# Reordering the first loads of a fused attention + token-mixing kernel: the first chunk of x as two column halves on two queues, and chunk 2 scaled in halves

## The chip, the cores and the metric

One core of a Trainium2 chip. The metric is the device time of one execution, in microseconds (us), lower is better; a profile gives the *span*, from the first to the last instruction of the program, which is some 2 us shorter than the time. All numbers are of fast runs (granted TensorE clock 1.0) unless said otherwise.

Names: PE is TensorE, DVE is VectorE, ACT is ScalarE, POOL is GpSimd, SP is SyncE, whose instruction stream issues most of the DMAs here. A load *lands* when the trace shows its completion.

## The reference, cut to what matters

```python
xn = _layernorm(x)                       # x: 2048 tokens x 1024, bf16
out = x + attention(xn, wq, wk, wv, wo, beta) + mixer(xn, w1, b1, w2, b2)

def mixer(x, w1, b1, w2, b2):            # mixes over the tokens
    h = _layernorm(x)
    u = gelu(einsum('bsd,sf->bdf', h, w1) + b1)     # contraction over the 2048 tokens
    y = einsum('bdf,fs->bds', u, w2) + b2
    return y.transpose(0, 2, 1)
```

What matters is the start of the mixer. The contraction runs over tokens, so the kernel takes x in 16 *chunks* of 128 tokens: chunk c must be loaded, its mean and variance found, its 1024 columns normalised to `h`, and then 8 matmuls (4 pieces of 128 columns of `w1`, times 2 halves of `h`) may use it.

## The kernel before: the parts that matter

The first loads, all issued from SP. Every `load_x` is 256 KB a chunk (128 rows of 2 KB), every `load_w1` 128 KB a chunk (rows of 1 KB).

```python
def loads(self):
    ...                                            # two memsets on GpSimd
    fw.op("act", lambda e: e.activation(..., ACT.Gelu_apprx_tanh), ...)   # loads the table early
    self.load_x(0, 1)
    self.load_x(1, 1)
    self.load_w1(0, 2)                             # chunks 0 and 1
    self.load_x(2, 1)
    self.load_x(3, 1)
    self.load_w1(2, 2)
    ...                                            # and so on
```

The statistics of chunks 1, 2, 4, 6, ... are two passes on ScalarE (one for the mean, one for the mean square); those of chunks 0, 3, 5, ... are `bn_stats` on VectorE. `scale` is two or three small operations (on GpSimd, but for chunk 0's first), the last a power of -0.5; `ln_h` is the normalisation on VectorE.

```python
ACT_STATS = (1, 2, 4, 6, 8, 10, 12, 14)

def norm_and_first_hidden(self):
    self.stats(0); self.scale(0)
    self.stats(1)
    self.ln_h(0, 0); self.ln_h(0, 1)               # in halves of 512 columns
    self.scale(1)
    self.ln_h(1, 0); self.ln_h(1, 1)
    self.early_hidden(0)                           # 8 matmuls
    self.stats(3)
    for c in self.ACT_STATS[1:]:
        self.stats(c)
    self.early_hidden(1)
    for c in range(2, N_TCH, 2):
        self.scale(c); self.ln_h(c)                # whole, 1024 columns
        if c + 3 < N_TCH: self.stats(c + 3, 0)
        self.scale(c + 1); self.ln_h(c + 1)
        if c + 3 < N_TCH: self.stats(c + 3, 1)
        ...
        self.early_hidden(c); self.early_hidden(c + 1)
```

In the traces here each engine works through its own instructions in the order in which they are written (in `hold_w1` below, VectorE waits until 9.23 us for chunk 3 and comes to chunk 2 at 10.57, although chunk 2's power is ready at 9.90). While the data arrives, 14 dummy matmuls keep TensorE busy.

The softmax here doesn't subtract the row's maximum and nothing guards it: scores larger than these inputs give would overflow.

## Time and profile before

| | before |
|---|---|
| time, median of 4 fast runs in the rounds of the comparison | 694.65 us (694.49 to 694.68) |
| span of the profiled run | 693.0 us |
| TensorE busy | 687.8 us, 99% |
| real matmuls begin | 6.58 us |
| TensorE's wait before chunk 2 | 1.02 us |
| chunk 2's first matmul | 11.22 us |

From the profile's page of the kernel before: span, busy time of each engine with its share of the span, and the chain of work that ended last by engine.

```profile
span 693.0 us, 11585 instructions
PE 687.8 (99%) x4822; PEld 329.1 (47%) x4822; DVE 268.4 (39%) x602; ACT 282.0 (41%) x513; POOL 118.2 (17%) x235
PE 98%; DMA 1%; ACT 0%; SPq 0%; DVE 0%; issue 0%
```

TensorE is the limit everywhere but in the first 12 us. The timeline of TensorE there (kernel before; columns: start, duration, engine, line, what, and in brackets the idle time before it and what ended it):

```profile
6.58 3.61 PE L217 MATMUL ps_all<-h,w1all 128*128 128x512 bf16 x16 [0.54 <-DVE h L836]
11.22 5.12 PE L217 MATMUL ps_all<-h,w1all 128*128 128x512 bf16 x23 [1.02 <-DVE h L836]
```

Chunks 0 and 1 are the 16 matmuls of the first line; then TensorE waits for the normalised chunk 2. The chain that ended last, in order of time (kernel before; columns: start, duration, what), says why:

```profile
2.19 4.92 DMA xin<-in_A_x_dram
...
7.14 1.16 ACT xn_tmp L800 x2
8.32 1.15 ACT xn_tmp L802 x2
9.47 1.05 ACT xn_tmp L800 x2
10.52 0.56 DVE h L836
11.22 662.61 PE ps_all L217 x4605
```

Chunk 2 of x, the fourth DMA, is issued at 2.19 us and lands at 7.12; ScalarE's two passes over it end at 9.47; then `h`, then 662 us of TensorE in one piece. One step is mislabelled. A wait is put down to the engine that came last, and the 1.05 us "ACT L800" is ScalarE's next pass, on another chunk. What really stands between ScalarE's end and VectorE's start is GpSimd, as its timeline line (kernel before) shows: a power that ends at 10.38, after a subtract that waited for ScalarE.

```profile
9.82 0.56 POOL L828 TENSOR_TENSOR ln_r<-ln_t,mhalf 128x1 f32<-128x1 f32 x1
```

ScalarE's timeline (kernel before) shows what released it: chunk 1's landing, then, after a pause of 0.68 us, chunk 2's.

```profile
4.13 1.06 ACT L800 ACTIVATE xn_tmp<-xin 128x1024 bf16<-128x1024 bf16 x1 [1.84 <-DMA xin<-in_A_x_dram]
...
6.28 0.19 ACT L802 ACTIVATION_READ_ACCUMULATOR xn_tmp<-xin 128x1 f32 x1
7.14 1.06 ACT L800 ACTIVATE xn_tmp<-xin 128x1024 bf16<-128x1024 bf16 x1 [0.68 <-DMA xin<-in_A_x_dram]
```

### The profile page before, as it was taken

How to read it: one execution, taken by the hardware profiler on the slowest of the kernel's cores; microseconds unless marked ns; L12 is line 12 of the kernel's file. 1: busy time of each engine (PE TensorE's matmuls, PEld its weight loads, DVE VectorE, ACT ScalarE, POOL GpSimd, SP SyncE). 2: the span in 40 equal slices, each digit the busy share in tenths (PEclk: the TensorE clock that was granted, in tenths of full speed). 3: DMA queues.
4: the chain of work that ended last, by engine and by line, in shares of the span. 5: the costliest groups of instructions: out<-in, count | busy, mean ns of one | idle time of the engine just before them, and what ended most of it. 6: DMA issues, size and time to landing. Idle time of an engine off the chain costs nothing.

```text
span 693.0 us, 11585 instructions
## 1 busy us (share of the span) xinstructions
PE 687.8 (99%) x4822; PEld 329.1 (47%) x4822; DVE 268.4 (39%) x602; ACT 282.0 (41%) x513; POOL 118.2 (17%) x235
## 2 busy tenths in 40 slices
PE   8999999999999999999999999999999999999998
PEld 3444444444444544545445454444445454444544
DVE  6731100000002433434555464655556463453545
ACT  7331111111136364454544525354543525443450
POOL 5810000000001221211212112121212212121230
PEclk9999999999999999999999999999999999999999
DMA  9377666323038445456272644526263442424114
GB/s 318 109 172 184 161 155 202 99 61 101 1 103 186 104 93 135 94 120 137 46 146 61 137 78 100 123 53 144 55 146 81 95 110 53 116 61 113 37 26 147
DMA packets 211325, 77.32 MB, mean 112 GB/s; under 512 B 173898, under 2 KB 203594, under 8 KB 211274
## 3 DMA queue, kind: packets, MB, share of 16 engines
q1 hardware_dynamic: 211274, 76.59, 44.7%
q8 instruction: 38, 0.62, 0.4%
q14 instruction: 13, 0.11, 0.1%
HBM read 59.79 MB, written 5.24 MB: 94 GB/s over the span
## 4 chain that ended last, share of the span: by engine, by line
PE 98%; DMA 1%; ACT 0%; SPq 0%; DVE 0%; issue 0%
PE ps_all L217 98%; DMA xin<-in_A_x_dram 1%; ACT xn_tmp L800 0%; SPq L245 0%; ACT xn_tmp L802 0%; DVE h L836 0%; DVE fin L1254 0%
## 5 line engine op out<-in xcount | busy, mean ns | idle before, releaser
L217 PE MATMUL ps_all<-gT,w2h 128*128 128x512 bf16 x896 | 229.0, 379 | 0.0
L1072 ACT ACTIVATE pT<-ps_all 128x512 bf16<-128x512 f32 x320 | 161.9, 617 | 111.3 <-PE ps_all L217 111.3
L217 PE MATMUL ps_all<-h,w1all 128*128 128x512 bf16 x896 | 193.7, 379 | 1.6 <-DVE h L836 1.6
L1080 POOL TENSOR_SCALAR_AFFINE_SELECT pT<-pT 128x256 bf16<-128x256 bf16 (+3 forms) x176 | 91.8, 527 | 545.0 <-ACT pT L1072 541.1
L217 PEld LDWEIGHTS ps_all<-h,w1all 128*128 128x128 bf16 x896 | 87.5, 98 | 107.7 <-issue 1.5
L217 PEld LDWEIGHTS ps_all<-gT,w2h 128*128 128x128 bf16 x896 | 79.9, 97 | 82.6 <-issue 7.8
L950 ACT ACTIVATE gT<-ps_all,bc 128x512 bf16<-128x512 f32 x56 | 37.7, 690 | 141.4 <-PE ps_all L217 141.4
L1118 DVE CAST ost<-ps_all 128x264 bf16<-128x264 f32 (+1 forms) x128 | 50.5, 396 | 80.4 <-PE ps_all L217 79.7
L217 PEld LDWEIGHTS ps_all<-vA,pT 128*128 128x128 bf16 x1280 | 50.3, 96 | 29.6 <-POOL pT L1080 0.5
L217 PE MATMUL ps_all<-xnT,wq 128*128 128x512 bf16 x256 | 60.5, 379 | 0.0
L217 PE MATMUL ps_all<-xnT,wk 128*128 128x512 bf16 x256 | 60.5, 379 | 0.0
L217 PE MATMUL ps_all<-wv_sb,xnT 128*128 128x512 bf16 x256 | 60.1, 379 | 0.0
L217 PE MATMUL ps_all<-vA,pT 128*128 128x33 bf16 x1280 | 51.7, 178 | 0.0
L977 DVE CAST qT<-ps_all 128x512 bf16<-128x512 f32 x29 | 20.1, 692 | 79.8 <-PE ps_all L217 79.8
L976 ACT ACTIVATE vA<-ps_all 128x512 bf16<-128x512 f32 x18 | 10.8, 599 | 90.6 <-PE ps_all L217 90.6
L888 DVE TENSOR_SCALAR gcol<-gcol 128x32 f32<-128x32 f32 x1 | 0.2, 181 | 118.6 <-ACT gcol L886 118.6
L217 PEld LDWEIGHTS ps_all<-wv_sb,xnT 128*128 128x128 bf16 x256 | 25.1, 98 | 30.2
L217 PEld LDWEIGHTS ps_all<-xnT,wk 128*128 128x128 bf16 x256 | 25.0, 98 | 30.2
L217 PEld LDWEIGHTS ps_all<-xnT,wq 128*128 128x128 bf16 x256 | 25.0, 98 | 30.1 <-issue 0.2
L976 ACT ACTIVATE kT<-ps_all 128x512 bf16<-128x512 f32 x32 | 19.1, 597 | 37.6 <-PE ps_all L217 37.6
L217 PE MATMUL ps_all<-wo_sb,oT 128*128 128x512 bf16 x128 | 34.3, 379 | 0.0
L961 DVE TENSOR_SCALAR etmp<-etmp 128x512 bf16<-128x512 bf16 x48 | 17.6, 367 | 39.0 <-ACT etmp L960 39.0
(68 smaller groups left out, 424.2 us busy)
## 6 DMA issues: line engine op xcount, KB each, us to landing
w2h<-in_B_w_dram SPq DMA_DIRECT2D x64, 224.0 KB, 3.2
w1all<-in_B_w_dram SPq DMA_DIRECT2D x12, 1024.0 KB, 5.3
wq<-in_A_wq_dram SPq DMA_DIRECT2D x32, 256.0 KB, 2.9
wk<-in_A_wk_dram SPq DMA_DIRECT2D x32, 256.0 KB, 2.9
stg<-in_A_x_dram SPq DMA_DIRECT2D x16, 256.0 KB, 3.8
out_dram<-stg SPq DMA_DIRECT2D x16, 256.0 KB, 2.9
xin<-in_A_x_dram SPq DMA_DIRECT2D x5, 512.0 KB, 7.4
w1all<-in_B_w_dram SPq DMA_DIRECT2D x8, 256.0 KB, 6.5
```

The source lines that it names most:

```text
L217: ins = self.nc.tensor.matmul(out, *args, **kwargs)
L888: fw.op("dve", lambda e: e.tensor_scalar(self.gcol[:], self.gcol[:], 1.0, None, op0=ALU.add), reads=[self.R_gcol], writes=[self.R_gcol])
L950: fw.op("act", lambda e: e.activation(self.gT[:, fc, half * 512:(half + 1) * 512], self.bank(b), ACT.Gelu_apprx_tanh, bias=self.b1c[:, fc: ...
L961: fl.op({"dve": (lambda e: e.tensor_scalar(et[:], et[:], 1.0, None, op0=ALU.min), 294, 330)}, [R_et], [R_et], prio=2)
L976: self.flow.op({"act": (lambda e, b: e.activation(dst, view(self.bank(b)), ACT.Copy), 635, 560), "dve": (lambda e, b: e.tensor_copy(dst, v ...
L977: "dve": (lambda e, b: e.tensor_copy(dst, view(self.bank(b))), 690, 727)},
L1072: fl.op({"act": (lambda e, b, slot=slot: e.activation(pT[:, slot, :], self.bank(b), ACT.Exp, scale=SCALE), 620, 530)}, [], [R[slot]], box= ...
L1080: fl.op({"pool": (lambda e, ap=ap, pat=pat: e.affine_select(ap, ap, pattern=pat, compare_op=ALU.is_ge, fill=0.0, base=0, channel_multiplie ...
L1118: fl.op({"dve": (lambda e, b: e.tensor_copy(dst, self.ps[:, b, 0:n * VW]), 150 + n * 35, 185 + n * 35)}, [], [self.R_ost[o][qb]], box=box, ...
```

## The change

The intent is to start the real matmuls sooner and to close the wait before chunk 2: chunk 0 arrives as two column halves issued at once from SP and from ScalarE; chunk 1 follows on ScalarE's queue; the first `w1` pieces come singly, so chunk 2 stands further ahead; chunk 2 is normalised, and taken by TensorE, in halves.

```diff
+        for half, issuer in ((0, "sp"), (1, "act")):
+            cols = slice(512 * half, 512 * half + 512)
+            fw.dma(self.xin[:, 0, cols], self.x_d[:, 0, cols], writes=[self.R_x0[half]], issuer=issuer)
+        self.load_x(1, 1, "act")
         fw.op("act", ... ACT.Gelu_apprx_tanh ...)
-        self.load_x(0, 1)
-        self.load_x(1, 1)
-        self.load_w1(0, 2)
+        self.load_w1(0, 1)
         self.load_x(2, 1)
+        self.load_w1(1, 1)
         self.load_x(3, 1)
+        self.load_x(4, 1)
         self.load_w1(2, 2)
 ...
         self.early_hidden(0)
-        self.stats(3)
         for c in self.ACT_STATS[1:]:
             self.stats(c)
+        self.stats(3, 0)
+        self.stats(3, 1, False)          # without the aggregate
+        self.scale(2)
+        self.ln_h(2, 0)
+        self.ln_h(2, 1)
+        self.aggregate(3)
         self.early_hidden(1)
         for c in range(2, N_TCH, 2):
-            self.scale(c)
-            self.ln_h(c)
+            if c > 2:
+                self.scale(c)
+                self.ln_h(c)
 ...
-        order = ... if c < 2 else \
+        order = ... if c < 3 else \      # half by half, so the first 4 matmuls need one half of h
```

(The rest is bookkeeping: which wait belongs to which half of chunk 0.)

More of the change, by code (lines that the diff above doesn't have):

```diff
@@ L632, in alloc @@
         self.R_xin = [Res(f"xin{c}") for c in range(N_TCH)]
+        self.R_x0 = [Res(f"x0_{half}") for half in range(2)]
         self.R_xnt = [Res(f"xnt{i}") for i in range(4)]
@@ L640, in over_early @@
         e = _Arena(self.nc, self.early_base, self.early_end)
-        wait = _after(*self.R_xin, *self.R_xnt)
+        wait = _after(*self.R_xin, *self.R_x0, *self.R_xnt)
         self.wv_sb = e.take("wv_sb", [P, N_DCH, D_MODEL], BF16)
@@ L717, in loads @@
         fw.op("pool", lambda e: e.memset(self.brow[:], 0.0), writes=[self.R_brow, self.R_brow2])
+        for half, issuer in ((0, "sp"), (1, "act")):
+            cols = slice(512 * half, 512 * half + 512)
+            fw.dma(self.xin[:, 0, cols], self.x_d[:, 0, cols], writes=[self.R_x0[half]], issuer=issuer)
+        self.load_x(1, 1, "act")
         fw.op("act", lambda e: e.activation(self.ln_t[:, 0, 0:1], self.mhalf[:, 0:1], ACT.Gelu_apprx_tanh),
               reads=[self.R_mhalf], writes=[self.R_st[0]], ns=1500)
-        self.load_x(0, 1)
-        self.load_x(1, 1)
-        self.load_w1(0, 2)
+        self.load_w1(0, 1)
         self.load_x(2, 1)
+        self.load_w1(1, 1)
         self.load_x(3, 1)
+        self.load_x(4, 1)
         self.load_w1(2, 2)
-        for c in range(4, 16, 2):
-            if c == 4:
-                self.load_x(4, 1)
-                self.load_x(5, 1)
-            else:
-                self.load_x(c, 2)
+        self.load_x(5, 1)
+        self.load_w1(4, 2)
+        for c in range(6, 16, 2):
+            self.load_x(c, 2)
             self.load_w1(c, 2)
@@ L742, in loads, with load_x, xin_half @@
         self.w1_next = 3
-    def load_x(self, c0, n):
+    def load_x(self, c0, n, issuer="sp"):
         self.fw.dma(self.xin[:, c0:c0 + n, :], self.x_d[:, c0:c0 + n, :],
-                    writes=[self.R_xin[c] for c in range(c0, c0 + n)])
+                    writes=[self.R_xin[c] for c in range(c0, c0 + n)], issuer=issuer)
+    def xin_half(self, c, half):
+        return self.R_x0[half] if c == 0 else self.R_xin[c]
     def load_w1(self, c0, n, issuer="sp"):
@@ L789, in norm_and_first_hidden, with stats @@
             self.early_hidden(c + 1)
-    def stats(self, c, part=None):
+    def stats(self, c, part=None, whole=True):
         fw = self.fw
@@ L806, in stats, with aggregate @@
         if part != 1:
-            fw.op("dve", lambda e: e.bn_stats(st[:, 0:6], src[:, 0:512]), reads=[self.R_xin[c]], writes=[R_t], ns=690)
+            fw.op("dve", lambda e: e.bn_stats(st[:, 0:6], src[:, 0:512]), reads=[self.xin_half(c, 0)], writes=[R_t], ns=690)
         if part != 0:
-            fw.op("dve", lambda e: e.bn_stats(st[:, 6:12], src[:, 512:1024]), reads=[self.R_xin[c], R_t], writes=[R_t],
+            fw.op("dve", lambda e: e.bn_stats(st[:, 6:12], src[:, 512:1024]), reads=[self.xin_half(c, 1), R_t], writes=[R_t],
                   ns=690)
-            fw.op("dve", lambda e: e.bn_aggr(self.ln_mv[:, c, :], st.rearrange("p (a s) -> p a s", s=6)),
-                  reads=[R_t], writes=[self.R_mean[c], self.R_var[c]])
+            if whole:
+                self.aggregate(c)
+    def aggregate(self, c):
+        st = self.ln_st[:, c, :]
+        self.fw.op("dve", lambda e: e.bn_aggr(self.ln_mv[:, c, :], st.rearrange("p (a s) -> p a s", s=6)),
+                   reads=[self.R_st[c]], writes=[self.R_mean[c], self.R_var[c]])
     def scale(self, c):
@@ L833, in ln_h @@
         a, z = (0, D_MODEL) if half is None else (512 * half, 512 * half + 512)
-        for hf in ((0, 1) if half is None else (half,)):
-            assert self.R_h[c][hf] is not None
         fw.op("dve", lambda e: e.tensor_scalar(self.h[:, c, a:z], self.xin[:, c, a:z], self.ln_mv[:, c, 0:1],
                                                self.ln_r2[:, c:c + 1], op0=ALU.subtract, op1=ALU.mult),
-              reads=[self.R_xin[c], self.R_mean[c], self.R_rs[c]],
+              reads=[self.xin_half(c, hf) for hf in ((0, 1) if half is None else (half,))]
+              + [self.R_mean[c], self.R_rs[c]],
               writes=self.R_h[c] if half is None else [self.R_h[c][half]], ns=(z - a) // 2 + 30)
@@ L843, in early_hidden @@
         last = c == N_TCH - 1
-        order = [(fc, half) for half in range(2) for fc in range(self.N_EARLY)] if c < 2 else \
+        order = [(fc, half) for half in range(2) for fc in range(self.N_EARLY)] if c < 3 else \
             [(fc, half) for fc in range(self.N_EARLY) for half in range(2)]
@@ L902, in ln_xn @@
                                                self.ln_r1[:, c:c + 1], op0=ALU.subtract, op1=ALU.mult),
-              reads=[self.R_xin[c], self.R_mean[c], self.R_r1], writes=[self.R_xnt[k]], ns=750)
+              reads=[self.xin_half(c, 0), self.xin_half(c, 1), self.R_mean[c], self.R_r1], writes=[self.R_xnt[k]], ns=750)
     def x_transpose(self, c):
```

## The prediction

> **What bounds the kernel now.** TensorE. The page has it busy 99% of a 693.0 us span, and the chain that ended last is 98% matmul. The change can only win idle TensorE time in the first 12 us. The timeline shows it: real matmuls begin at 6.58 us, 16 of them (chunks 0 and 1) run, then TensorE waits 1.02 us for the normalised chunk 2 (DVE h) and starts again at 11.22 us; after that the chain is one unbroken 662 us piece. Only what brings that piece forward counts: about 1 us, 0.15%, is on offer.
>
> **What sets 11.22 us.** The chain: chunk 2 of x, fourth transfer on the one queue, lands at 7.12 us. ScalarE has been free since 6.47 us; its two passes end at 9.47, GpSimd's subtract and power at 10.38, VectorE's 128x1024 scaling runs 10.52 to 11.07, first matmul 11.22.
>
> **What the change does, costed.**
> 1. Chunk 0 in halves on two queues. It lands at 3.46 us now; 2.56 us of VectorE and GpSimd work follow before h. The Trainium skill (DMA: Bandwidth & Descriptors, section "Issuing engines are not separate DMA queues") says that both queues run on the same 16 engines, and the windows show those near full (365 GB/s between 2.5 and 3.5 us), so I expect only 0.2 to 0.4 us. The first w1 piece lands at 6.42 us, just when h is ready; halved and put second it stops mattering. First real matmul near 6.2 to 6.3.
> 2. Chunk 1 on ScalarE's queue. By that page's section "Queues, rings and completion order" the queues alternate packet by packet, so it now shares with w1's packets: 4.11 us becomes 4.2 to 4.6. Its matmuls start no earlier, perhaps 0.2 later. ScalarE's table load (1.28 us) moves about 0.9 us later, hidden before that landing.
> 3. Chunk 2 has 896 KB up to its end instead of 1024: at the 0.65 us per 256 KB between later landings, 0.3 us earlier. ScalarE begins it near 6.8 instead of 7.14.
> 4. Chunk 2 scaled in halves (about 0.37 us instead of 0.55) and taken half by half: 0.2 us more. Chunk 2's matmuls start near 10.7 instead of 11.22.
> 5. The cost: chunk 3's aggregate (0.21 us) now stands behind both halves of chunk 2. From an aggregate's end to its scaling the timeline shows 1.0 to 1.4 us (GpSimd add and power), then 0.55 us of scaling. So h of chunk 3 is ready 2.6 to 2.9 us after chunk 2's scaling begins, while TensorE has finished chunk 2 after 2.2. I expect a NEW wait of 0.3 to 0.6 us before chunk 3, which gives most of the gain back: chunk 3's matmuls start near 12.8 against 12.9.
>
> Afterwards TensorE is saturated as before. Net: about 0.3 us gained, 694.4 us, certainly within 2%. The range is wide for so small a term because the emission order of the attention part comes from a modelled clock that the change also moves.
>
> **What would show it.** Right: first real matmul near 6.2; chunk 2's first near 10.7; a new wait on DVE h before the 25th real matmul; TensorE's busy time unchanged. Step 3 is wrong if ScalarE's chunk 2 starts at 7.1 or later; step 5 if TensorE runs without a gap from chunk 2 on, and the gain is then 0.5 us or more.
>
> **What would make it wrong.** Chunk 1 delayed beyond 4.8 us by slow first w1 packets (then chunk 2 is late too, and the change loses); much earlier landings through two queues filling the first 2.5 us, which now move only 66 to 193 GB/s (then nearly 1 us is won); a different attention schedule.

## The result, and the profile after

| | before | after |
|---|---|---|
| time, median of 4 fast runs | 694.65 us (694.49 to 694.68) | 694.93 us (694.78 to 695.29) |
| chunk 0 lands | 3.46 | 3.45 and 3.63 (halves) |
| chunk 1 lands | 4.11 | 4.94 |
| chunk 2 lands | 7.12 | 5.51 |
| ScalarE begins chunk 2 | 7.14 | 7.20 |
| TensorE: first real matmul / chunk 2 / chunk 3 | 6.58 / 11.22 / 12.94 | 6.63 / 11.12 / 13.11 |

The ratio of times is 1.0005, with a 95% interval of 0.9988 to 1.0023: the same within 2%, and by itself not told apart from no change. (Ratios are the mean time of one kernel's fast runs over that of the other's of the same rounds, so not quite the ratio of the medians quoted.) The forecast was a gain of 0.3 us; the medians say a loss of 0.28. The time is within the 2% that the prediction's text allows, the sign is not what was predicted.

The page of the changed kernel:

```profile
span 693.2 us, 11590 instructions
PE 688.0 (99%) x4822; PEld 329.0 (47%) x4822; DVE 268.5 (39%) x603; ACT 281.7 (41%) x513; POOL 117.9 (17%) x235
PE 98%; ACT 1%; DMA 1%; DVE 0%; POOL 0%; issue 0%; ACTq 0%; DVEq 0%
```

TensorE's timeline (changed kernel), to be held against the two lines above:

```profile
6.63 1.89 PE L217 MATMUL ps_all<-h,w1all 128*128 128x512 bf16 x8 [0.69 <-DVE h L851]
8.90 1.89 PE L217 MATMUL ps_all<-h,w1all 128*128 128x512 bf16 x8 [0.38 <-DVE h L851]
11.12 5.19 PE L217 MATMUL ps_all<-h,w1all 128*128 128x512 bf16 x22 [0.33 <-DVE h L851]
```

There is a new hole in front of chunk 1. A second new hole hides in the third line: the start of the 17th real matmul is 11.12, that of the 25th (chunk 3) 13.11, so 1.99 us for 8 matmuls that take 1.72 elsewhere. The page does not list it, as a matmul's end is modelled and pipelined; the chain that ended last does (changed kernel):

```profile
1.24 3.70 DMA xin<-in_A_x_dram
...
4.96 1.16 ACT xn_tmp L812 x2
...
6.14 1.15 ACT xn_tmp L814 x2
7.29 1.05 ACT xn_tmp L812 x2
...
8.36 1.15 ACT xn_tmp L814 x2
9.51 1.05 ACT xn_tmp L812 x2
10.56 0.73 DVE h L851 x2
11.29 0.13 DVE ln_mv L828
...
11.50 0.26 POOL ln_t L843
...
11.83 0.58 POOL ln_r L845
...
12.51 0.56 DVE h L851
...
13.11 660.89 PE ps_all L217 x4597
```

Before, the chain began with the landing of chunk 2. Now it begins with the landing of chunk **1** at 4.94 us, and runs without a pause through ScalarE. Chunk 2, which now lands 1.6 us earlier, is no longer in it. ScalarE's timeline (changed kernel) shows chunk 2 begun straight after chunk 1, without a wait on a DMA:

```profile
4.96 1.06 ACT L812 ACTIVATE xn_tmp<-xin 128x1024 bf16<-128x1024 bf16 x1 [1.73 <-DMA xin<-in_A_x_dram]
...
7.10 0.18 ACT L814 ACTIVATION_READ_ACCUMULATOR xn_tmp<-xin 128x1 f32 x1
7.20 1.04 ACT L812 ACTIVATE xn_tmp<-xin 128x1024 bf16<-128x1024 bf16 x1
```

Then the chain passes through chunk 3's aggregate (L828), GpSimd's add and power, and chunk 3's scaling: the aggregate moved behind chunk 2.

**Everything after the head is unchanged.** TensorE's instructions come in the same order in both programs (but for chunk 2's own 8 matmuls, now half by half), and the start of the last matmul is 677.43 to 677.45 us after chunk 3's first in every fast profile: 690.37 - 12.94 = 677.43 before, 690.55 - 13.11 = 677.44 after. So "when does chunk 3 start" is the whole question, and the possible attention reshuffle is out.

### The profile page after: what moved, and what is told of

Read it like the earlier page. It is cut to its first block, busy times and chain, and to the rows that moved or that the text cites. A ratio compares the mean times of both kernels' runs of the same rounds, so it can differ in the third digit from the quotient of the medians.

```text
span 693.2 us, 11590 instructions
## 1 busy us (share of the span) xinstructions
PE 688.0 (99%) x4822; PEld 329.0 (47%) x4822; DVE 268.5 (39%) x603; ACT 281.7 (41%) x513; POOL 117.9 (17%) x235
## 4 chain that ended last, share of the span: by engine, by line
PE 98%; ACT 1%; DMA 1%; DVE 0%; POOL 0%; issue 0%; ACTq 0%; DVEq 0%
PE ps_all L217 98%; DMA xin<-in_A_x_dram 1%; ACT xn_tmp L812 0%; ACT xn_tmp L814 0%; DVE h L851 0%; POOL ln_r L845 0%; ACTq L245 0%; DVE fin L1270 0%; POOL ln_t L843 0%; DVE ln_mv L828 0%; DVEq L65 0%
```

## Experiments

**Theory A.** Two things happened in the head. Chunk 1, on ScalarE's queue, takes turns with what SP's queue moves and lands late; as ScalarE works through chunks 1 and 2 in order, that takes away what the earlier landing of chunk 2 should have given. And chunk 3's late aggregate costs TensorE 0.27 us before chunk 3. **Theory B**, the rival: the loads do help, and the moved aggregate alone eats the gain. Inside theory A there are again rivals for *why* chunk 1 is late: slow first packets of `w1`, sharing with anything, or ScalarE's queue being slow by itself.

Twelve sets ran, of eleven kernels, each 5 times in rounds with the kernel before. TensorE's order of work is that of before in all of them (chunk 2's halves apart). The effects are tenths of a microsecond in 694, every interval includes a ratio of 1. I therefore read three things together: the medians, the mean spans (the kernel before came out at 692.67 to 692.68 on three chips, 9 runs each; but its four fast runs in the next experiment at 692.83, so the mean of one set of four or five can be off by 0.15), and the landings in the profile.

### The noise floor: before against before

No edit.

> The kernel before against itself: the noise floor. Any theory: ratio 1.000 within 0.0004; second profile with chunk 1 landing near 4.1 us, ScalarE's chunk 2 near 7.1, TensorE's chunk 2 at 11.2 us, if those numbers are no accident of one execution.

One of the five executions ran at a granted clock of 0.754 and took 886.71 us. The profile fell on that one, so it is not used. The four fast ones have a median of 694.69 against 694.54 in the same rounds: two sets of runs of one kernel can differ by 0.15 us.

### The loads alone, and the compute order alone

`loads_only` is the changed kernel with `norm_and_first_hidden` and the matmul order of before; `compute_only` is the changed kernel with the loads of before.

```diff
 # loads_only                              # compute_only
-        self.stats(3, 1, False)            -  two halves of chunk 0, chunk 1 on ScalarE's queue
-        self.scale(2); self.ln_h(2, 0) ... -  single w1 pieces
+        (order of before)                  +  self.load_x(0, 1); self.load_x(1, 1); self.load_w1(0, 2); ...
```

> The changed loads with the compute order of before. Theory A (the late landing of chunk 1 on ScalarE's queue pushes ScalarE back and cancels the earlier chunk 2): chunk 1 lands near 4.9, ScalarE starts chunk 2 near 7.2 although it landed near 5.5, TensorE's chunk 2 starts near 11.25 and its chunk 3 follows without a wait: time that of before, 0 to +0.1 us. Theory B (the loads help and the moved aggregate eats it): TensorE's chunk 2 starts below 10.9 and the kernel is 0.3 us or more faster than before.

> The loads of before with the changed compute order (chunk 2 in halves, aggregate of chunk 3 behind them). Theory A: ScalarE as before, chunk 2 at 7.14; TensorE's chunk 2 starts 0.1 to 0.15 earlier (11.1), then waits 0.3 before chunk 3, which starts near 13.1 against 12.9: about 0.2 us slower than before. Theory B predicts the same wait, so the size of the loss (0.2, or 0.4 and more) against loads_only tells which part of the 0.28 us is whose.

`loads_only`: 694.66 us against 694.54; mean span 692.78 against 692.68, so 0.1 us slower, which is within the scatter of such sets. Chunk 1 lands at 4.69, chunk 2 at 5.37, and ScalarE begins chunk 2 only at 6.95, 2.24 us after chunk 1. Its profile has chunk 2's matmuls at 11.01 and chunk 3's at 12.73, without a wait between. Theory B, which wanted chunk 2 below 10.9 and a gain of 0.3 us from the loads, is not borne out. `compute_only`: 694.50 us; mean span 692.62 against 692.68: level, where I had expected 0.2 us lost. Its profile does show the expected wait (chunk 2 at 10.75, chunk 3 at 12.74, 1.99 us apart) but ScalarE began chunk 2 at 6.80 in it, not at 7.14: chunk 2 had landed at 6.78 although its loads are those of before. That is a first sign that landings differ between executions by as much as the effects looked for.

### The aggregate back in front

```diff
-        self.stats(3, 1, False)
+        self.stats(3, 1)
...
         self.ln_h(2, 1)
-        self.aggregate(3)
```

> The changed kernel with chunk 3's aggregate put back before chunk 2's scaling; loads untouched. Both theories: the wait of 0.3 us before chunk 3 goes. Theory A: TensorE's chunk 2 still starts near 11.1 and runs on, so 0.1 us faster than before and about 0.3 us faster than the changed kernel. If the wait stays or moves to chunk 4 or 5, another term is missing.

694.76 us against 694.54. In its profile the wait before chunk 3 is gone, as both theories say: the chain goes from chunk 2 straight into one piece of TensorE (chain of this experiment's kernel):

```profile
10.90 0.41 DVE h L850
...
11.45 662.61 PE ps_all L217 x4605
```

Chunk 3 follows at 13.18, 1.73 us later. But chunk 2 starts at 11.45 there, since chunk 1 landed at 5.27 in this execution. The mean span is 692.74, against 692.86 and 692.90 for the two sets of the changed kernel. So undoing the move wins 0.12 to 0.16 us of the span, not the 0.3 I expected. That is no more than the scatter of such sets; what is shown is that the wait is gone. With the late aggregate undone the loads still bring no gain on the kernel before (692.74 against 692.68), which speaks against theory B once more.

### Chunk 1 back on SP's queue

```diff
-        self.load_x(1, 1, "act")
+        self.load_x(1, 1)
```

> The changed kernel with one thing undone: chunk 1 is issued on the SP queue, ahead of the first w1 piece (ScalarE's queue carries the half chunk 0 only). Theory A (ScalarE's statistics are serial, 2.34 us a chunk from the landing of chunk 1, and set TensorE's chunk 2): chunk 1 lands at 4.1 to 4.4 instead of 4.7 to 5.3, ScalarE starts chunk 2 at 6.5 to 6.8, TensorE's chunk 2 starts near 10.5, waits 0.3 to 0.5 for the late aggregate, chunk 3 at 12.5: 0.4 us faster than before, 0.6 faster than the changed kernel. Rival (TensorE's chunk 2 hangs on something else, such as VectorE's order): still 11.0 or later.

Chunk 1 lands at 4.17 and ScalarE begins it at 4.20. But now ScalarE waits for chunk 2 again, which lands at 6.80 (timeline of ScalarE, this experiment):

```profile
4.20 1.06 ACT L812 ACTIVATE xn_tmp<-xin 128x1024 bf16<-128x1024 bf16 x1 [1.47 <-DMA xin<-in_A_x_dram]
...
6.82 1.06 ACT L812 ACTIVATE xn_tmp<-xin 128x1024 bf16<-128x1024 bf16 x1 [0.29 <-DMA xin<-in_A_x_dram]
```

Chunk 2 starts at 10.76, so the rival's "11.0 or later" fails; chunk 3 is at 12.76. The time is 694.71 against 694.54, the mean span 692.68, level with before and 0.2 us shorter than the changed kernel's. The expected 0.4 us did not come: with one more DMA ahead of it on its queue than in the changed kernel, chunk 2 was not there in time, and the late aggregate took its 0.27 (10.76 to 12.76 is 2.00).

### Chunk 2 ahead of w1

```diff
-        self.load_w1(0, 1)
         self.load_x(2, 1)
+        self.load_w1(0, 1)
```

> The changed kernel with chunk 2 ahead of the first w1 piece on the SP queue; chunk 1 stays on ScalarE's queue and now alternates with warm 2 KB packets of x. If the first packets of w1 are what makes chunk 1 late: it lands at 4.4 to 4.6. If sharing the engines with anything does it: 4.7 or later, as chunk 2 has twice the bytes of the w1 piece. The w1 piece itself lands later, near 5.5 to 6.2.

The clearest loss: 695.48 us against 694.54 (ratio 1.0012, interval 0.9998 to 1.0025), mean span 693.48. Chunk 1 lands at 5.77, just behind chunk 2, which took turns with it and lands at 5.59; the `w1` piece lands at 5.97. ScalarE starts late and runs without a pause, 2.24 us from chunk 1 to chunk 2 (its timeline, this experiment):

```profile
5.80 1.06 ACT L812 ACTIVATE xn_tmp<-xin 128x1024 bf16<-128x1024 bf16 x1 [2.57 <-DMA xin<-in_A_x_dram]
...
8.04 1.04 ACT L812 ACTIVATE xn_tmp<-xin 128x1024 bf16<-128x1024 bf16 x1
```

So it is not only the first packets of `w1` that can delay chunk 1: with twice the bytes of another load next to it, it came later still. How much later, this profile overstates: it is the slowest of the five executions. The packet records in the trace (no view here shows them) have 16 closing packets for each load; 15 of chunk 1's had started by 4.67 us, against 4.10 to 4.62 in the four profiles with the loads of the change, but the last only at 5.27. The mean span puts the typical landing near 5.2 (an estimate: 693.48 - 680.09 - 1.99 - 3.92 - 2.26, terms as under "What adds up"), against 4.62 for the changed kernel by the same reckoning. This is the sharpest evidence for the theory: chunk 2, the load that was thought critical, landed at 5.59 instead of 7.12, and the kernel lost nearly 1 us.

### Holding the other queue back

```diff
-        self.load_w1(0, 1)
+        self.load_w1(0, 1, extra=[self.R_x0[0].w])     # SP waits for the first half chunk
```

> The changed kernel, but the SP queue holds the first w1 piece and all behind it until the first half chunk has landed (a wait added, nothing else). Sharing theory (chunk 1 is late because w1 and chunk 2 on the other queue take turns with it): chunk 1 lands at 4.1 to 4.3 although it is still on ScalarE's queue behind the half chunk. Second-queue theory (ScalarE's queue is slow by itself): still 4.7 or later. Chunk 2 is then issued near 4.0 and lands near 6.3 to 6.8, so the kernel gains at most 0.3 us on the changed one.

The edit only adds a wait. Chunk 1 lands at 4.41, between the two forecasts: with the other queue held it is 0.13 to 0.32 us later than as the second load of SP's queue (4.09 to 4.28 in the five fast profiles in which chunk 1 stands on SP's queue and ScalarE's carries no more than the half chunk), and 0.05 to 0.86 earlier than in the four profiles with the loads of the change (4.46, 4.69, 4.94, 5.27). The packet records tell the two theories apart better than the landing: 15 of chunk 1's 16 closing packets had started by 3.71 us, no later than in the five profiles on SP's queue (3.71 to 3.91) and well before the 4.10 to 4.62 of the four. Only the last came late, at 4.10. So, in this one profile, holding SP's queue takes the delay away for 15 of the 16 parts, as the sharing theory says; that ScalarE's queue costs anything by itself is not shown, and why one part came late is open.

The time was 695.07 us against 694.64, for a reason I had not expected. VectorE, which works in order, stood waiting for chunk 3 (landed at 9.21) before it could scale chunk 2, whose power was ready at 9.90 (timeline of VectorE, this experiment):

```profile
9.23 0.69 DVE L819 BATCH_NORM_STATS2 ln_st<-xin 128x6 f32<-128x512 bf16 x1 [0.68 <-DMA xin<-in_A_x_dram]
...
10.57 0.72 DVE L851 TENSOR_SCALAR h<-xin,ln_mv,ln_r 128x512 bf16<-128x512 bf16 x2
```

### Chunk 1 first on ScalarE's queue

```diff
-        two halves of chunk 0 on two queues
+        self.load_x(0, 1)
         self.load_x(1, 1, "act")
```

(with the aggregate in front)

> Chunk 0 whole first on the SP queue, chunk 1 whole first on ScalarE's queue at the same time, w1 and chunk 2 behind chunk 0; aggregate in front. Both land near 4.0 if they simply share. Then first matmul near 7.0, ScalarE's chunk 2 at 6.4, TensorE's chunk 2 at 10.3 to 10.5 right behind chunk 1: 0.6 to 0.8 us faster than before. If the second queue is slow by itself, chunk 1 lands clearly after chunk 0.

A miss. They share, but land at 4.28 (chunk 0) and 4.46 (chunk 1), not near 4.0, and the kernel is 0.64 us slower than before (695.18 against 694.54). Chunk 0, 0.8 us later than before, holds up VectorE, which is serial too (its timeline, this experiment):

```profile
4.30 0.69 DVE L816 BATCH_NORM_STATS2 ln_st<-xin 128x6 f32<-128x512 bf16 x1 [3.11 <-DMA xin<-in_A_x_dram]
...
10.56 0.21 DVE L825 BATCH_NORM_AGGREGATE ln_mv<-ln_st 128x2 f32<-128x12 f32 x1
10.69 0.72 DVE L848 TENSOR_SCALAR h<-xin,ln_mv,ln_r 128x512 bf16<-128x512 bf16 x2
```

GpSimd had chunk 2's power ready at 9.94, but VectorE came to chunk 2 only at 10.69.

### Chunks in order on SP's queue, w1 on ScalarE's

```diff
-        two halves of chunk 0 on two queues; self.load_x(1, 1, "act")
+        self.load_x(0, 1); self.load_x(1, 1)
         fw.op("act", ... ACT.Gelu_apprx_tanh ...)
-        self.load_w1(0, 1); self.load_x(2, 1); self.load_w1(1, 1)
+        self.load_w1(0, 1, "act"); self.load_w1(1, 1, "act"); self.load_x(2, 1)
```

(with the aggregate in front)

> Chunks 0, 1, 2, 3 on the SP queue in order of need; the first two w1 pieces on ScalarE's queue, issued behind its table load so that their packets begin near 3.3 us; aggregate in front. If only the packets ahead of chunk 1 count: chunk 1 at 4.1 to 4.3, chunk 2 below 6.0, ScalarE without a pause (chunk 2 at 6.4 to 6.5), TensorE's chunk 3 near 12.1: 0.3 to 0.5 us faster than before in the same rounds. If two queues at once always delay chunk 1, it lands near 4.7 and the gain is gone.

I had the issue time wrong: the two `w1` loads were issued at 0.95 and 1.37 us, while ScalarE was still in its table load (0.80 to 2.08). So `w1` took turns with chunks 0 and 1 after all, and chunk 1 landed at 4.46, as in the experiment before this one. ScalarE began chunk 2 at 6.72, chunk 3's matmuls were at 12.37. The time was 694.39 against 694.64, a gain of 0.25 us by the medians, just below what was expected, and of 0.13 by the mean spans (692.54 against 692.67). So a second queue does not cost time as such: here it carries `w1` and no chunk of x.

### One queue, single w1 pieces

```diff
-        two halves of chunk 0 on two queues; self.load_x(1, 1, "act")
+        self.load_x(0, 1); self.load_x(1, 1)
         self.load_w1(0, 1); self.load_x(2, 1); self.load_w1(1, 1); ...     # as in the change
-        self.stats(3, 1, False) ... self.aggregate(3)
+        self.stats(3, 1)
```

It keeps from the change the single `w1` pieces (chunk 2 has 896 KB up to its end) and the halves of chunk 2, and drops the second queue and the late aggregate.

> Chunks 0 and 1 whole, all on the SP queue as before; only the w1 pieces single, so that chunk 2 stands in front of w1's second; chunk 2 in halves and the aggregate in front of them. Theory A: chunk 1 at 4.1, chunk 2 by 6.4, ScalarE runs through (4.1, 6.5), TensorE's chunk 2 near 10.3 to 10.5 and no wait before chunk 3 (12.0 to 12.2): 0.6 to 0.8 us faster than before. If w1's first packets hold chunk 2 back to 6.8, only 0.4.

694.25 us against 694.54, mean span 692.40 against 692.67. Chunk 1 lands at 4.09, chunk 2 at 6.16, before ScalarE is free, so ScalarE runs through (4.12, then 6.35). TensorE's chunk 3 starts at 12.13, as expected, but the gain is half of what was expected: 0.6 to 0.8 was reckoned from the profile of before, whose chunk 3 (12.94) was late for its kernel, by the estimate under "What adds up". Against `agg_first`, which differs only in the first loads (chunks 0 and 1 with ScalarE's queue in play), the mean span is 0.34 us shorter (692.40 against 692.74, on different chips): the most direct measure here of what the second queue cost. It ran once more on another chip:

> The best version so far once more, to see whether its 0.3 us repeats: 0.2 to 0.4 us faster than before, chunk 1 at 4.1, ScalarE's chunk 2 at 6.3 to 6.6, TensorE's chunk 3 near 12.1 to 12.4. If it comes out level with before, the gain was chance of one set of rounds.

694.27 against 694.64; mean span 692.40 against 692.67, the same 0.27 us. Its chain has no DMA and no ScalarE in it any more; from 1.25 us on it is TensorE's own work, the dummy matmuls included (chain of the second run):

```profile
1.25 9.09 PE ps_all L217 x30
10.35 0.11 issue
10.46 662.61 PE ps_all L217 x4605
```

A small hole of 0.27 us is left between chunks 1 and 2 (487 ns from the last matmul of chunk 1 to the first of chunk 2, where 216 is usual); the chain's "issue" of 0.11 is all that the profile makes of it.

### The changed kernel again, beside these

> The changed kernel again, on the chip and in the rounds of the next three. Chunk 1 lands between 4.7 and 5.3 us again, ScalarE's chunk 2 starts 2.24 us after its chunk 1, TensorE's chunk 3 near 13.1 with a wait of 0.27 us in front: 0.2 to 0.3 us slower than before.

695.00 us against 694.64: 0.36 us slower by the medians, mean span 692.86 against 692.67, so 0.19. The loss repeats. But the profiled execution was a lucky one: chunk 1 landed at 4.46, ScalarE began chunk 2 at 6.72, TensorE ran through chunks 0 to 2 and waited only before chunk 3 (12.64, 1.97 us after chunk 2 at 10.67).

### What adds up

In the four profiles with the loads of the change, ScalarE's chunk 2 begins 2.23 to 2.24 us after its chunk 1, whatever chunk 1's landing was. With that the two orders can be written down:

| | before | changed |
|---|---|---|
| ScalarE begins chunk 2 | when chunk 2 lands | chunk 1's landing + 0.02 + 2.24 |
| from there to chunk 2's first matmul | 4.08 (whole) | 3.92 (halves) |
| from there to chunk 3's first matmul | 1.72 | 1.99 (aggregate behind) |
| rest of the span | 680.09 | 680.09 |

The last row is the span minus chunk 3's start (693.03 - 12.94 and 693.20 - 13.11; 680.07 to 680.10 in every fast profile). From the second row on, the new compute order costs 3.92 + 1.99 - 4.08 - 1.72 = +0.11 us. For the loads, the mean spans give estimates of the typical execution, as they were not all profiled: the kernel before starts chunk 3 at 692.67 - 680.09 = 12.58, so ScalarE begins chunk 2 at 6.78; the changed kernel at 692.88 (mean of its two sets) - 680.09 = 12.79, so ScalarE begins chunk 2 at 6.88 and chunk 1 lands near 4.62. That splits the 0.21 us of the mean spans into +0.10 for the loads and +0.11 for the order. The separate runs gave +0.10 (`loads_only`) and -0.06 (`compute_only`) in mean span; the second does not show its 0.11, and a run set's scatter is as large as that, so the split is an estimate and not shown.

The estimates also say that the profile of before was an unlucky draw. It has chunk 2 at 7.12; the typical execution, by this estimate, has it near 6.76. Its span of 693.03 is in the upper tail: 5 of that kernel's 31 fast runs in the experiments reached 693.0.

One remainder stays open. Time minus span is 2.09 us on average in the changed kernel (9 runs), and 1.94 in the kernel before (27 runs). So about 0.15 us of the 0.28 to 0.36 by the medians lie outside the span, where no view reaches. `agg_first`, `x1_on_sp`, `hold_w1` and `w1_later` have it too (2.09 to 2.11), `loads_only` does not (1.89), so it is not simply the second queue.

## Why the prediction was right or wrong, point by point

The time lay within 2%, as said. That is no merit: the first 12 us, all that was in play, are 1.7% of the time. The central number and its sign were wrong: -0.3 us was forecast, +0.28 came. The forecast was also more than its steps add up to: they have chunk 3 at 12.8 against 12.9, and since nothing after it moves, that is 0.1 us and not 0.3.

- **What bounds the kernel, and that only the unbroken piece counts: right.** 677.43 to 677.45 us from chunk 3's first to the last matmul in every fast profile.
- **Step 1 (chunk 0 sooner by 0.2 to 0.4): wrong.** The halves landed at 3.45 and 3.63 against 3.46 whole; the first real matmul was at 6.63 instead of 6.2. The argument used was right and should have been taken further. The Trainium skill (DMA: Bandwidth & Descriptors, section "Issuing engines are not separate DMA queues") says that DMAs from both issuers run on the same 16 engines and only issue time is saved; this trace agrees for chunk 0, which had nothing queued ahead of it and so no issue time to save.
- **Step 2 (chunk 1 from 4.11 to 4.2 to 4.6): right in kind, mis-sized, and in the profiled run this is the term that failed.** 4.94 in this profile; 4.46 to 5.27 in four. The same page's section "Queues, rings and completion order" has each DMA engine go round between queues packet by packet; that fits the landings here (chunk 1 and the first `w1` piece landed within 0.4 us of each other in all four), and in `w1_later`, with chunk 2 as its neighbour, chunk 1 came at 5.77. I counted only the `w1` piece of 128 KB as its rival, not the later loads on SP's queue: by the packet records of this profile SP's queue started 227 KB between chunk 1's first packet and its last.
- **Step 3 (ScalarE begins chunk 2 near 6.8): wrong by its own test.** It began at 7.20. I computed the landing of chunk 2, which came even earlier than I said (5.51 against about 6.8), and overlooked that ScalarE would not be free: it needs 2.24 us from the start of chunk 1, and chunk 1 was late. With a landing of 4.2 to 4.6, as step 2 had it, ScalarE would have been free at 6.5 to 6.9, so step 3 fell with step 2. A gain on the old critical load was spent on delaying the load in front of it.
- **Step 4 (0.2 us from the halves): about right.** 4.08 to 3.92 is 0.16.
- **Step 5 (a new wait of 0.3 to 0.6 before chunk 3): right in kind, a little large.** 0.27 us (1.99 instead of 1.72); it goes when the aggregate stands in front (`agg_first`, 1.73).
- **What would make it wrong:** "chunk 1 delayed beyond 4.8 us ... then chunk 2 is late too, and the change loses" is what happened in the profiled run. The cause named there, slow first `w1` packets, is not needed: with chunk 2 of x beside it instead, chunk 1 was later.
- **The baseline, which no step questions: by the estimate, this turned the sign.** Every step starts from the profile of before, with chunk 3 at 12.94, and that execution was slow for its kernel. For the changed kernel the prediction said "near 12.8"; the estimate from its nine spans is 12.79. For the kernel before the estimate is 12.58, not 12.94. So the typical start of chunk 3 in the changed kernel was forecast well, and what it was compared with was 0.36 us too late. This rests on the spans of executions that were not profiled, so it is an estimate, not shown.

## What to carry to other kernels

When a load is on the critical chain, look at the engine that will use it: if that engine works through several inputs in order, the landing of its *first* input counts too, and giving a later one bandwidth at the first one's cost can lose time. Here the second DMA queue undid the order of need that one queue keeps (chunk 1 landed at 4.46 to 5.27 us in place of 4.09 to 4.28), and the same compute order ran 0.34 us shorter with the chunks on one queue. And before trusting a tenth of a microsecond read from one profile, look at a second one: landings alone moved by 0.3 to 0.8 us between executions of the same loads, and a baseline that is late by as much promises a gain that is not there.

## What the Trainium skill lacked or had wrong

- DMA: Bandwidth & Descriptors, section "Rules for kernel authors", says that spreading DMAs over SP and ScalarE for bandwidth does not help. In the first microseconds it did here. The windows view between 3.5 and 4.5 us, kernel before (columns: stretch, its length, busy time and count of PE, weight loads, VectorE, ScalarE and GpSimd, granted clock, DMA share, and last GB/s):

```profile
3.50:4.50 1.00, 1.00 (x4) 0.30 (x3) 0.96 (x2) 0.37 (x1) 0.00 (x0) 1.00 0.78 203
```

  The same window of the changed kernel:

```profile
3.50:4.50 1.00, 1.00 (x5) 0.33 (x4) 0.90 (x2) 0.00 (x0) 0.00 (x0) 1.00 1.02 382
```

  And of `one_queue`:

```profile
3.50:4.50 1.00, 1.00 (x4) 0.32 (x3) 0.97 (x2) 0.38 (x1) 0.00 (x0) 1.00 0.67 171
```

  With one queue the rate falls to 203 and 171 GB/s there (285 and 304 in two other executions with one queue, so these are low draws), with two it stays at 382 (347 to 389 in the seven profiles with two queues loading freely), and the first 1024 KB had landed by 5.96 us instead of 7.12 (5.90 to 6.16 in the four profiles with these loads, 6.50 in both with one queue and single pieces). It gained nothing because, as argued above, the wrong chunk paid for it. What the dip of the single queue is made of was not settled.
- The same page says how queues alternate, but not how late the last part of one load can then be: in `w1_later` 15 of chunk 1's 16 closing packets had started by 4.67 us and the last at 5.27.
- No page gives the scatter of a landing between executions: chunk 1 landed at 4.46 to 5.27 us in four executions with the same first loads, chunk 2 at 6.78 and 7.12 in two with the loads of before (in different rounds, some on different chips).
